# Four re-orderings in a kernel of linear attention and a gated feed-forward block

## Chip and metric

One core of a Trainium2 chip. The metric is the device time of one execution in microseconds, the median of several runs. The engines are TensorE (PE; its weight loads are listed as PEld), VectorE (DVE), ScalarE (ACT), GpSimd (POOL) and SyncE (SP), which here only issues DMAs.

## What is computed

The reference, cut to what matters (8 batches, 8 heads, 576 positions, head size 64; then 4608 tokens, model width 512, hidden width 1536):

```python
def phi(x, c, s):
    r = np.maximum(x, 0.0)
    return np.concatenate([r * c, r * s], axis=-1)
q_p, k_p = phi(q, cos_w, sin_w), phi(k, cos_w, sin_w)
kv = np.einsum('bhsf,bhsd->bhfd', k_p, v)
z = np.sum(k_p, axis=2)
num = np.einsum('bhsf,bhfd->bhsd', q_p, kv)
den = np.einsum('bhsf,bhf->bhs', q_p, z)[..., None] + 1e-06
x = (num / den).transpose(0, 2, 1, 3).reshape(B * S, H * D)

g, val = x @ w_gate, x @ w_val
out = (0.5 * g * (1.0 + erf(g / sqrt(2))) * val) @ w_out
```

## The kernel before

The tokens are taken in nine blocks of 512 (n = 0 to 8), the hidden width in twelve units of 128 columns (jt = 0 to 11, called steps here). A batch has 576 tokens, so a block is made of the end of one batch and the beginning of the next. While the feed-forward part of block n runs, the attention of batch n + 1 is computed in between, and batch n + 2 is loaded and prepared. The order on every engine is the order in which the program is written; the framework only adds the waits.

**Attention of a batch.** `load` brings q, k and v in, two DMAs each, on SyncE's queue (LOADS says in which step). `prep` and `prep_both` multiply the positive part by cosine or sine, one position index j at a time (j = 0 to 8): `prep_both` does q and k in one instruction, on VectorE (L193) or ScalarE (L191). `cast_v` makes v bf16 (L208). `turn_q` transposes q's features with two DMAs (L222). `kv_unit` (L270) sums k times v. `nm_unit` makes the numerators and denominators of one tile of 128 tokens in PSUM banks 6 and 7 (L311), divides on VectorE (denominator L322, reciprocal L323, product into x_sb L324), and `turn_x` transposes x_sb into xT by DMA (L378), in two pieces where a tile falls into two blocks. Tiles that fall into the next block are called late; they are turned in one go. All these transposes, loads and the stores of the output go through SyncE's one queue in the order written. COMING (block 3) and PREPS (blocks 4 to 6) say in which step what is prepared.

**Gate and value.** In blocks 1 to 3, `gv_unit` computes a unit: four matmuls for the gate, GELU on ScalarE (L439), four for the value, and gate times value into hT on VectorE (L442). It alternates between banks 0, 1 and 2, 3. The first `heads` units of a block are done in two halves of 256 columns, all first halves ahead of all second halves, since the block's last columns arrive late. From block 4 on, pairs of units are computed by Strassen's scheme in Winograd's form, with seven products p1 to p7 instead of eight (class `Pair`, matmuls L649). p1 writes a sum bank and ScalarE copies it to another bank (L668); p5 goes to bank 3 (MIX) and is copied to SBUF (L672); p6 is added to the sum bank, and VectorE adds the copy of p5 (L676); p2 and p3 complete the two gates (GELU L681, L685); p7 and p4 complete the two values (L689; products into hT L690, L694). The sums of x that this needs (`x_sum`, L629) are made on GpSimd. Blocks 4 and 5 have four groups each (`group`): one such pair and one ordinary unit, with three steps' worth of other work in between; blocks 6 to 8 have pairs alone (`fast_step`).

**Output.** The output of block n - 1 is computed in the steps of block n (`o_step`), in two parts p of 256 tokens, each by seven products (`product`, matmuls L547) in six steps: products 1 and 2, then 5, 6, 7, 4, 3 (2 and 1 first up to block 3). Products 1, 2, 4, 6 and 7 write bank 4: 1, 6 and 7 accumulate in its left half u, 2 and 4 go to its right half v. Products 5 and 3 write bank 5. After products 1, 6 and 7 ScalarE copies the partial sum u to SBUF (L564), and VectorE adds copies and banks to the output tile (L560). The sums of hT that this needs (`h_sum`, L529) are made on GpSimd from block 4 on.

The order inside a group, with its numerators:

```python
f.p1();  numerators(n, 3 * g);      f.p5();  x()
f.p6();  numerators(n, 3 * g + 1);  f.p2();  y()
f.p3();  f.p7(MIX)
# then an ordinary unit; between its gate and its value:
numerators(n, 3 * g + 2);  z();  f.p4()
```

x, y and z are the steps 3g, 3g + 1 and 3g + 2: an output product, the attention work of the step (where x_sb tiles are turned), and sums on GpSimd.

Of the kernel before, what the change touches and what calls it, by code (L numbers as in the profile page):

```python
# [9 lines left out]
FP32 = mybir.dt.float32  # L10
# [6 lines left out]
def kernel(  # L17
# [13 lines left out]
    nc = tc.nc  # L31
# [6 lines left out]
    JT = J // 128  # L38
# [381 lines left out]
    def gv_unit(n, jt, c0=0, w=BLK, to=None, between=None):  # L420
        xt = xT[n]
        js = slice(jt * 128, (jt + 1) * 128)
        if to is None:
            to = (0, 1) if turn[0] % 2 == 0 else (2, 3)
            turn[0] += 1
        if n not in hT:
            hT[n] = ffn.tile([128, JT, BLK], BF16, name="hT")
        for g, wt in ((0, wg_sb), (1, wv_sb)):
            for ct in range(CT):
                nc.tensor.matmul(  # L430
                    bank(to[g])[:, 0:w],
                    lhsT=wt[:, ct, js],
                    rhs=xt[:, ct, c0:c0 + w],
                    start=(ct == 0),
                    stop=(ct == CT - 1),
                )
            if g == 0:
                gel = ffn.tile([128, BLK], FP32, name="gel")
                nc.scalar.activation(gel[:, 0:w], bank(to[0])[:, 0:w], AF.Gelu)  # L439
                if between:  # L440
                    between()
        nc.vector.tensor_mul(  # L442
            hT[n][:, jt, c0:c0 + w], gel[:, 0:w], bank(to[1])[:, 0:w]
        )
# [36 lines left out]
    JH, CH = JT // 2, C // 2  # L481
# [22 lines left out]
    def place(n, p, name, cols, dtype):  # L504

        if name[0] == "u":
            if n < NB - 1:
                at = {"u1": 0, "u6": 1, "u7": 2}[name] * CH
                return sm[:, at:at + CH]
            rest[0] += CH  # L510
            late = phis.rearrange("p a m r f -> p (a m r f)").bitcast(FP32)
            return late[:, rest[0] - CH:rest[0]]
        at = (int(name[1]) - 1) * JH * 128
        if n < NB - 1:
            return sm[:, 3 * CH:].bitcast(BF16)[:, at:at + JH * 128]
        late = st[:, p].rearrange("p m x -> p (m x)").bitcast(BF16)
        return late[:, at:at + JH * 128]
# [17 lines left out]
    got = {}  # L535
    LEFT, RIGHT = slice(0, CH), slice(CH, C)

    def product(n, p, i, u, m, v):


        a, b = PROD[i]
        key = n, p
        at = {1: u, 6: u, 7: u, 5: m, 3: m, 2: v, 4: v}[i]
        last = n == NB - 1
        joint = not last and n > 2
        for j in range(JH):
            nc.tensor.matmul(  # L547
                at,
                lhsT=hs.setdefault(key, h_parts(n, p))[a][:, j],
                rhs=ts[b][:, j],  # L550
                start=(j == 0 and i in ((1, 2, 4, 5), (1, 4, 5))[joint]),
                stop=(j == JH - 1),
                skip_group_check=i in (3, 6, 7) or joint and i == 2,
            )
        if key not in got:
            got[key] = [outp.tile([128, C], FP32, name="o_sb") for _ in range(2)]
        lo, hi = got[key]

        def add(o, k, x, op=ALU.add):
            nc.vector.tensor_tensor(o, got[key, k], x, op=op)  # L560

        if i in (1, 6, 7) or last and i == 5:
            got[key, i] = place(n, p, f"u{i}", CH, FP32)
            nc.scalar.copy(got[key, i], at)  # L564
        if i == (2 if last or joint else 1):
            add(lo[:, LEFT], 1, v)
        if i == 7:
            add(hi[:, RIGHT], 7, got[key, 5] if last else m)
        if i == 4:
            add(hi[:, LEFT], 7, v, ALU.subtract)  # L570
        if i == 3:
            add(lo[:, RIGHT], 6, m)
        if last and p == 1:

            if i == 2:
                store((nc.sync, nc.sync), 4 * n + p, lo, 0, CH)
            if i == 4:
                store((nc.sync, nc.gpsimd), 4 * n + 2 + p, hi)
            if i == 3:
                store((nc.sync, nc.scalar), 4 * n + p, lo, CH, C)  # L580
        elif i in (3, 4):
            flush()
            stores.append((4 * n + 2 + p, hi) if i == 4 else (4 * n + p, lo))
            if last:
                flush()
# [311 lines left out]
    def js(a, b):  # L897
        return tuple(range(a, b))
# [7 lines left out]
        },  # L906
        3: {
            0: [("k", 4, js(6, 9)), ("v", 4, 0)], 1: [("v", 4, 2)],
            6: [("qk", 5, js(0, 2))], 7: [("qk", 5, js(2, 3))], 8: [("qk", 5, js(3, 5))],
            9: [("v", 5, 0), ("qk", 5, js(5, 6))], 10: [("v", 5, 2), ("qk", 5, js(6, 8))],  # L910
            11: [("qk", 5, js(8, 9))],
        },
    }
    LOADS = {
        (1, 11): [(3, "k"), (3, "v")],
        (2, 1): [(4, "q")], (2, 6): [(4, "k"), (4, "v")],
        (2, 11): [(5, "k")], (3, 1): [(5, "q")], (3, 2): [(5, "v")],
        (3, 9): [(6, "q", 0, 4), (6, "k", 0, 4)],
        (4, 0): [(6, "q", 4, R), (6, "k", 4, R)], (4, 1): [(6, "v")],
        (4, 8): [(7, "q", 0, 4), (7, "k", 0, 4), (7, "v")],  # L920
# [60 lines left out]
    for n in range(1, 4):  # L981
        b = n + 1

        t_kv, t_nm, t_turn = {1: (7, 9, 12), 2: (6, 7, 11), 3: (2, 5, 9)}[n]
        for jt in range(JT):
            if n == 1 and jt >= t_nm:
                nm_unit(2, jt - t_nm, (6, 4, 6)[jt - t_nm])
                turn_x(2, jt - t_nm)
            heads = (0, 2, 4, 2)[n]
            if jt >= heads:  # L990
                gv_unit(n, jt)
            else:
                for i in range(2):
                    half, unit = divmod(2 * jt + i, heads)
                    gv_unit(n, unit, half * HALF, HALF)
                    if n == 1:
                        j = JA + 2 * jt + i
                        prep("q", b, 1, (j,), eng=nc.scalar)
                        prep("q", b, 0, (j,))
                        if jt == i == 0:  # L1000
                            turn_x_pe(1, 3, 5, act_copy)
            if n > 1:
                o_step(n, jt)
            elif jt % 3 == 1:
                flush()
            if n == 1 and jt == 2:
                prep("q", b, 0, (R - 1,))
                prep("q", b, 1, (R - 1,), eng=nc.scalar)
                turn_q(b)
                nm_unit(1, NT - 1)  # L1010
            if n == 1 and jt == 3:
                turn_x(1, NT - 1)
            nms = [(b, jt - t_nm)] if n > 1 and 0 <= jt - t_nm < NT else []
            if n == 2 and jt < 2:
                nms.append((n, 3 + jt))

            i = jt - t_nm - 1
            if n > 1 and 0 <= i < late_of(b):
                turn_x(b, i)
            for bt in nms:  # L1020
                nm_unit(*bt)
            if jt == t_kv:
                kv_unit(b)
            if n == 1 and jt in (2, 3, 4):
                prep_third("k", b, jt - 2)
            if n == 1 and jt == 5:
                cast_v(b, 0, 4, dve_copy)
            if (n, jt) in q3:
                cosines, sines_ = q3[n, jt]
                prep("q", 3, 1, sines_, eng=nc.scalar)  # L1030
                prep("q", 3, 0, cosines)
            for name, c, what in COMING.get(n, {}).get(jt, ()):
                if name == "v":
                    cast_v(c, what, what + 2, dve_copy)
                elif name == "qk":
                    for j in what:
                        prep_both(c, 0, j, nc.scalar if j % 2 else nc.vector)
                        prep_both(c, 1, j, nc.scalar)
                else:
                    prep(name, c, 0, what)  # L1040
                    prep(name, c, 1, what, eng=nc.scalar)
            c = {(2, 1): 2}.get((n, jt), b if n > 1 and jt == t_turn else None)
            if c is not None and n < 3:
                turn_q(c + 1)
            start_loads(n, jt)
            if c is not None:
                for i in range(late_of(c), NT):
                    turn_x(c, i)
            if (n, jt) == (3, JT - 1):
                turn_q(b + 1)  # L1050
            if n == 1 and 4 <= jt < 8:
                wo_sum(("T3", "T1", "T2", "T4")[jt - 4])
            more(n, jt)
# [7 lines left out]
    turns = []  # L1061

    def numerators(n, jt):
        b, t = n + 1, {5: 0, 6: 1, 7: 2, 9: 3, 10: 4}.get(jt)
        if t is not None:
            nm_unit(b, t)
            turns.append((b, t))
# [42 lines left out]
    for n in range(4, NB):  # L1110
# [4 lines left out]
        for i, T in enumerate(pairs):  # L1115
            new = Pair(n, T, 2 * (made % 2), 1, made % 2)
            made += 1
            at = 3 * groups + 2 * i
# [16 lines left out]
    for what in (  # L1135
# [3 lines left out]
        if isinstance(what, str):  # L1139
            p = "ST".index(what[0])  # L1140
# [33 lines left out]
```

## Time and profile before

| | |
|---|---|
| runs | 321.83, 322.48, 325.06 us; median 322.48 |
| the profiled execution | 323.84 us, of which the span is 321.8 |
| busy: PE, PEld | 300.5 us (93%), 222.4 us (69%) |
| busy: DVE, ACT, POOL | 236.3 (73%), 190.1 (59%), 136.9 us (43%) |
| chain of work that ended last, by engine | PE 53%, DMA 19%, DVE 9%, issue 6%, ACT 6%, SP queue 3%, POOL 2% |
| granted TensorE clock | 0.99 |

The page's times are microseconds from the start of the span. Block 3 runs from about 114 to 150, block 4 to 185, block 5 to 219, and blocks 6 to 8 to about 302. A line of a timeline gives start, duration, engine, line, operation, output and inputs, shape, count, and in brackets the idle time before it and what ended that. Matmuls overlap: four of 256 columns are listed with 0.60 us but follow each other every 0.44 us, four of 512 columns every 0.86, and an output product of six takes 0.66.

### The profile page before, as it was taken

How to read it: one execution, taken by the hardware profiler on the slowest of the kernel's cores; microseconds unless marked ns; L12 is line 12 of the kernel's file. 1: busy time of each engine (PE TensorE's matmuls, PEld its weight loads, DVE VectorE, ACT ScalarE, POOL GpSimd, SP SyncE). 2: the span in 40 equal slices, each digit the busy share in tenths (PEclk: the TensorE clock that was granted, in tenths of full speed). 3: DMA queues.
4: the chain of work that ended last, by engine and by line, in shares of the span. 5: the costliest groups of instructions: out<-in, count | busy, mean ns of one | idle time of the engine just before them, and what ended most of it. 6: DMA issues, size and time to landing. Idle time of an engine off the chain costs nothing.

```text
span 321.8 us, 7828 instructions
## 1 busy us (share of the span) xinstructions
PE 300.5 (93%) x3014; PEld 222.4 (69%) x3039; DVE 236.3 (73%) x511; ACT 190.1 (59%) x393; POOL 136.9 (43%) x116
## 2 busy tenths in 40 slices
PE   8799999999999999968998999899999999999993
PEld 3574455654866676635776777677888888888883
DVE  5664887899897996659578947884778765756681
ACT  7664676957473853177566757584555465554631
POOL 5675450000000000008846487747992867296320
PEclk9799999999999999999999999999999999999998
DMA  7999999883799979999799998428641411113035
GB/s 274 229 187 256 298 333 370 250 127 60 248 170 221 346 138 155 294 257 201 92 270 226 322 139 239 84 57 122 94 85 36 89 33 35 42 25 65 3 75 123
DMA packets 71126, 53.66 MB, mean 167 GB/s; under 512 B 45393, under 2 KB 58449, under 8 KB 71089
## 3 DMA queue, kind: packets, MB, share of 16 engines
q1 hardware_dynamic: 61312, 41.17, 56.9%
q0 software_dynamic: 9696, 11.93, 16.0%
q8 instruction: 24, 0.39, 0.5%
q14 instruction: 14, 0.11, 0.1%
q10 hardware_dynamic: 80, 0.07, 0.1%
HBM read 37.75 MB, written 9.44 MB: 147 GB/s over the span
## 4 chain that ended last, share of the span: by engine, by line
PE 53%; DMA 19%; DVE 9%; issue 6%; ACT 6%; SPq 3%; POOL 2%; POOLq 0%; ACTq 0%; DVEq 0%
PE ps L649 22%; PE ps L547 14%; PE ps L430 13%; DMA st<-in_q_dram 7%; DMA wo_sb<-in_moe_w_out_dram 4%; DMA st<-in_v_dram 2%; DMA qT<-phis 2%; DMA wv_sb<-in_moe_w_val_dram 2%; SPq L222 2%; PE ps L311 2%; DVE x_sb L324 2%; DVE hT L442 2%; PE ps L270 2%; DMA xT<-x_sb 1%; ACT sm L564 1%
## 5 line engine op out<-in xcount | busy, mean ns | idle before, releaser
L430 PE MATMUL ps<-xT,wv_sb 128*128 128x512 bf16 (+1 forms) x245 | 56.5, 351 | 0.2
L430 PE MATMUL ps<-xT,wg_sb 128*128 128x512 bf16 (+1 forms) x230 | 54.1, 349 | 1.6 <-DMA xT<-x_sb 0.6
L629 POOL TENSOR_TENSOR fs<-xT 128x512 bf16<-128x512 bf16 x10 | 12.0, 1204 | 99.9 <-DVE phis L193 98.1
L439 ACT ACTIVATE gel<-ps 128x512 f32<-128x512 f32 (+1 forms) x62 | 33.5, 542 | 28.6 <-PE ps L430 26.8
L442 DVE TENSOR_TENSOR hT<-gel,ps 128x512 bf16<-128x512 f32 (+1 forms) x62 | 37.7, 614 | 16.4 <-PE ps L430 13.5
L529 POOL TENSOR_TENSOR sm<-hT 128x768 bf16<-128x768 bf16 x20 | 32.8, 1641 | 30.0 <-PE ps L649 16.3
L430 PEld LDWEIGHTS <-wv_sb 128*128 128x128 bf16 x248 | 24.2, 98 | 20.9
L547 PEld LDWEIGHTS <-sm 128*128 128x128 bf16 x336 | 32.9, 98 | 7.2
L560 DVE TENSOR_TENSOR o_sb<-sm,ps 128x256 f32<-128x256 f32 x56 | 23.3, 417 | 17.5 <-ACT sm L564 13.6
L547 PEld LDWEIGHTS <-hT 128*128 128x128 bf16 x288 | 28.0, 98 | 11.2 <-issue 6.3
L649 PE MATMUL ps<-fs,ws 128*128 128x256 bf16 x240 | 34.5, 273 | 1.2 <-ACT ps L668 1.0
L649 PEld LDWEIGHTS <-ws 128*128 128x128 bf16 x320 | 30.2, 98 | 6.2 <-ACT ps L668 1.7
L689 DVE TENSOR_TENSOR ps<-fs,ps 128x512 f32<-128x512 f32 x26 | 18.1, 695 | 21.7 <-PE ps L649 15.5
L177 ACT ACTIVATE phis<-st,sin_t 128x256 bf16<-128x256 f32 (+1 forms) x75 | 31.5, 483 | 3.2 <-DMA st<-in_q_dram 2.3
L430 PEld LDWEIGHTS <-wg_sb 128*128 128x128 bf16 x248 | 22.6, 98 | 15.5 <-issue 0.5
L649 PE MATMUL ps<-xT,wg_sb 128*128 128x256 bf16 x208 | 31.2, 273 | 0.0
L681 ACT ACTIVATE gel<-ps 128x512 f32<-128x512 f32 x26 | 15.5, 597 | 26.0 <-PE ps L649 26.0
L547 PE MATMUL ps<-wo_sb,hT 128*128 128x256 bf16 x192 | 25.3, 272 | 4.6 <-ACT sm L564 4.6
L324 DVE TENSOR_TENSOR x_sb<-ps,rec 128x512 bf16<-128x512 f32 x38 | 26.3, 691 | 1.3
L685 ACT ACTIVATE gel<-ps 128x512 f32<-128x512 f32 x26 | 15.5, 598 | 12.5 <-PE ps L649 10.0
L547 PE MATMUL ps<-T,sm 128*128 128x256 bf16 x168 | 22.9, 273 | 0.0
L547 PE MATMUL ps<-wo_sb,sm 128*128 128x256 bf16 x168 | 22.9, 273 | 0.0
(123 smaller groups left out, 562.6 us busy)
## 6 DMA issues: line engine op xcount, KB each, us to landing
out_dram<-o_sb SPq DMA_DIRECT2D x69, 128.0 KB, 2.4
st<-in_v_dram SPq DMA_DIRECT2D x12, 576.0 KB, 7.0
st<-in_k_dram SPq DMA_DIRECT2D x8, 576.0 KB, 5.1
st<-in_q_dram POOLq DMA_DIRECT2D x4, 576.0 KB, 12.0
st<-in_q_dram SPq DMA_DIRECT2D x4, 576.0 KB, 4.9
st<-in_q_dram SPq DMA_DIRECT2D x3, 640.0 KB, 5.9
st<-in_q_dram SPq DMA_DIRECT2D x3, 512.0 KB, 4.2
wg_sb<-in_moe_w_gate_dram POOLq DMA_DIRECT2D x6, 256.0 KB, 7.3
```

The costliest lines, as they stand in the source:

```text
L177: nc.scalar.activation(o, i, AF.Relu, scale=tab[:, j:j + 1])
L324: nc.vector.tensor_tensor(x, nm[:, :, :, 0:D], rec[:, :, :, None].to_broadcast([128, 2, 4, D]), op=ALU.mult,)
L430: nc.tensor.matmul(bank(to[g])[:, 0:w], lhsT=wt[:, ct, js], rhs=xt[:, ct, c0:c0 + w], start=(ct == 0), stop=(ct == CT - 1),)
L439: nc.scalar.activation(gel[:, 0:w], bank(to[0])[:, 0:w], AF.Gelu)
L442: nc.vector.tensor_mul(hT[n][:, jt, c0:c0 + w], gel[:, 0:w], bank(to[1])[:, 0:w])
L529: eng.tensor_tensor(a[name][:, j0:j1], a[x][:, j0:j1], a[y][:, j0:j1], op=op)
L547: nc.tensor.matmul(at, lhsT=hs.setdefault(key, h_parts(n, p))[a][:, j], rhs=ts[b][:, j], start=(j == 0 and i in ((1, 2, 4, 5), (1, 4, 5))[ ...
L560: nc.vector.tensor_tensor(o, got[key, k], x, op=op)
L649: nc.tensor.matmul(to[:, 256 * half:256 * half + 256], lhsT=w_part(a, j * 128, (j + 1) * 128)[:, ct], rhs=xb[self.n][b][:, ct], start=(hal ...
L681: nc.scalar.activation(self.gel0, self.other, AF.Gelu)
L685: nc.scalar.activation(gel1, bank(MIX), AF.Gelu)
L689: nc.vector.tensor_tensor(bank(val), self.m5, self.sum, op=ALU.add)
```

## The change

It has four parts, and touches no size and no type.

```diff
@@ product
-        if i in (1, 6, 7) or last and i == 5:
-            got[key, i] = place(n, p, f"u{i}", CH, FP32)
-            nc.scalar.copy(got[key, i], at)
+        if i in (6, 7) or i == (2 if joint else 1) or last and i == 5:
+            k, of = (1, u) if i == 2 else (i, at)
+            got[key, k] = place(n, p, f"u{k}", CH, FP32)
+            nc.scalar.copy(got[key, k], of)
@@ COMING and LOADS
-            6: [("qk", 5, js(0, 2))], 7: [("qk", 5, js(2, 3))], 8: [("qk", 5, js(3, 5))],
-            9: [("v", 5, 0), ("qk", 5, js(5, 6))], 10: [("v", 5, 2), ("qk", 5, js(6, 8))],
-            11: [("qk", 5, js(8, 9))],
+            5: [("qk", 5, js(0, 1))], 6: [("qk", 5, js(1, 2))], 7: [("qk", 5, js(2, 4))],
+            8: [("v", 5, 0), ("qk", 5, js(4, 5))], 9: [("v", 5, 2), ("qk", 5, js(5, 7))],
+            10: [("qk", 5, js(7, 9))],
-        (2, 11): [(5, "k")], (3, 1): [(5, "q")], (3, 2): [(5, "v")],
+        (2, 11): [(5, "k")], (3, 0): [(5, "q")], (3, 1): [(5, "v")],
@@ the loop over blocks 1 to 3
-            heads = (0, 2, 4, 2)[n]
+            heads = (0, 2, 4, 4)[n]
             if jt >= heads:
-                gv_unit(n, jt)
+                gv_unit(n, jt, to=(2, 6) if (n, jt) == (3, JT - 1) else None)
...
             start_loads(n, jt)
+            c = {(2, 1): 2, (3, 2): 3, (3, 9): 4}.get((n, jt))
             if c is not None:
                 for i in range(late_of(c), NT):
                     turn_x(c, i)
@@ numerators (blocks 4 and 5)
-        b, t = n + 1, {5: 0, 6: 1, 7: 2, 9: 3, 10: 4}.get(jt)
+        b, t = n + 1, {5: 0, 7: 1, 8: 2, 10: 3, 11: 4}.get(jt)
```

1. **Copy.** For the outputs of blocks 3 to 7 (`joint`; ten parts) the copy of the first sum u is issued behind product 2 instead of between products 1 and 2.
2. **Loads.** Batch 5's q and v are loaded one step earlier (steps 0 and 1 of block 3), and the late tiles of batch 3 are turned in step 2 of block 3 instead of step 11 of block 2. On SyncE's queue the order after batch 5's k was: two late transposes, a store of two DMAs, q, v. It is now: q, the store, v, the two late transposes. The preparation of batch 5 begins in step 5 instead of 6 and ends in step 10 instead of 11; v's casts move from steps 9 and 10 to 8 and 9.
3. **Block 3's units.** Four units instead of two are done in halves. The last unit (11) writes banks 2 and 6 instead of 0 and 1.
4. **Numerators.** In blocks 4 and 5 the five tiles are done in steps 5, 7, 8, 10, 11 instead of 5, 6, 7, 9, 10. On SyncE's queue tile 4's transpose moves from ahead of a store to just ahead of the transpose of the next batch's q.

GpSimd's order of instructions stays as it was. TensorE has 16 matmuls more.

## The prediction

> **What bounds the kernel now.** I read first the list of TensorE's waits: engine, line, releaser, total us, times, longest.
>
> ```profile
> PE ps L547 <- ACT sm L564: 4.6, 10, 0.5
> PE ps L311 <- DVE x_sb L324: 3.5, 3, 2.8
> ...
> PE ps L649 <- ACT ps L668: 1.0, 1, 1.0
> ...
> PE ps L430 <- DMA xT<-x_sb: 0.6, 2, 0.3
> ```
>
> These four come to 9.7 us, and each is touched by a part of the change. (p1 to p7 are the seven products of a pair of hidden units, products 1 to 7 those of the output.) Whether a wait's removal reaches the end shows in the busy time by stretch (PE, weight loads, DVE, ACT, POOL, clock, DMA share, GB/s):
>
> ```profile
> 140.00:160.00 20.00, 16.05 (x183) 10.98 (x185) 15.36 (x28) 14.32 (x28) 13.20 (x9) 1.00 0.90 167
> ...
> 200.00:220.00 20.00, 18.86 (x171) 14.41 (x171) 17.23 (x38) 13.26 (x24) 10.11 (x8) 1.00 0.39 84
> ...
> 260.00:280.00 20.00, 19.54 (x180) 17.29 (x178) 13.88 (x25) 11.12 (x21) 8.60 (x8) 1.00 0.19 40
> ```
>
> From 222 us TensorE is the only full engine; in blocks 4 and 5 (150 to 219) VectorE is close behind; at 140 to 160 nobody is full, so something is waited for. TensorE's timeline (start, duration) shows the waits:
>
> ```profile
> 117.61 0.60 PE L430 MATMUL ps<-xT,wg_sb 128*128 128x256 bf16 x4 [0.28 <-DMA xT<-x_sb]
> ...
> 142.40 0.42 PE L311 MATMUL ps<-kv_sb,qT 128*128 128x65 bf16 x8 [2.76 <-DVE x_sb L324]
> ...
> 152.08 0.61 PE L649 MATMUL ps<-fs,ws 128*128 128x256 bf16 x4 [0.99 <-ACT ps L668]
> ...
> 236.32 0.82 PE L547 MATMUL ps<-wo_sb,hT 128*128 128x256 bf16 x6
> 237.59 0.82 PE L547 MATMUL ps<-wo_sb,hT 128*128 128x256 bf16 x6 [0.46 <-ACT sm L564]
> ```
>
> The last two lines are output products 1 and 2, with one of the ten 0.46 us waits between them.
>
> The chain of waits behind the 2.76 us, and SyncE's queue ahead of it:
>
> ```profile
> 132.49 5.57 DMA st<-in_q_dram
> ...
> 138.79 1.32 ACT phis L191 x2
> 140.11 0.49 ACT gel L439
> ```
> ```profile
> 125.39 1.89 SPq L98 DMA_DIRECT2D st<-in_k_dram  x2
> 127.41 3.13 SPq L378 DMA_TRANSPOSE xT<-x_sb  x2
> 130.59 1.22 SPq L453 DMA_DIRECT2D out_dram<-o_sb  x2
> 131.92 1.05 SPq L98 DMA_DIRECT2D st<-in_q_dram  x2
> ```
>
> Batch 5's q lands at 138.06. The feature preparation waits for it in the queues of ScalarE and VectorE, and a GELU and a numerator stand behind it there.
>
> The profiled execution took 323.84 us: span 321.8, 2.04 around it. The median of the runs is 322.48, 1.36 less. I sum against 323.84 and carry the difference to the median.
>
> **The copy of the first sum.** Products 1 and 2 write the two halves of one PSUM bank; product 2 now waits until the copy (0.37 us) has read the first half. The copy moves behind product 2. The next write to the copied half is product 6, two steps later, so nobody on TensorE waits for it there; on ScalarE the GELU of p3 is queued behind, whose matmuls end 0.44 us after product 2, when the copy is done. The vector add behind the copy loses nothing: before, it could start at 0.46 + 0.66 = 1.12 us after product 1, now at 0.66 + 0.42 = 1.08. What is late next for product 2 is its fifth matmul, which reads the last hidden tiles of the block: VectorE ends them at 252.28, and that matmul would start at 252.13 + 0.44 = 252.57. It fits. Ten waits of 0.46: six from 221 us on count in full (2.76), two in the first groups of blocks 4 and 5, where VectorE idles (0.92); the two in their third groups are counted with the numerators. Sum 3.7.
>
> **Batch 5's q.** Its two loads pass two transposes and go out after k's, at 127.3 and 127.9 instead of 131.9 and 132.5. Bounds of the landing: 127.9 + 5.1 (k's own time) = 133.0, and 127.9 + 8.6 (the slowest v load there) = 136.5. I take 134.2: k and q together are 2.36 MB, and the two best slices here moved 388 and 371 GB/s, which is 6.2 us from 128, when the transposes of batch 4's q let go. The store, v and the late transposes follow, these to about 134 instead of 130.5; they land within the 8.6 too, and their first reader is POOL's x sum at 144.84.
>
> But the first preparation also moves a step earlier, from step 6 to 5, where VectorE arrives at 132.5 and ScalarE at 130.2. After the landing come sine 0.72, GELU 0.49, product into hT 0.60, output add 0.33, a Strassen sum 0.47, and 0.08 + 0.24 + 0.70 for the numerator: 3.6. TensorE wants the bank back at 136.84, so a landing after 133.2 makes it wait, one for one. At 134.2: 1.0 instead of 2.76. Gain 1.75 (0 to 2.76).
>
> **Unit 11 in banks 2 and 6.** Block 4's first copy (L668, p1 into bank 1) no longer waits for unit 11's hT (151.38). It then follows its own matmuls: copy 0.57 + 0.1, of which 0.44 lies beside p5, so 0.25 of the 0.99 stays. ScalarE now carries three preparations (3 x 0.62) beside GELU and copy in steps 9 and 10, 2.6 us in a step of 2.64; I charge 0.15 for unit 10's GELU, since unit 11 wants its bank. Gain 0.6 (0 to 0.99). With no preparation left in step 11, q's transpose for batch 5 starts earlier than 153.5.
>
> **Four halved units.** 16 matmuls more, but eight of 256 columns take 0.88 us and four of 512 take 0.86: 4 x 0.02 = 0.08 us. GELU grows by 4 x 0.39 - 2 x 0.59 = 0.4 and the hT products by 4 x 0.416 - 2 x 0.683 = 0.3; VectorE's 2.31 us of idle at 125.76 hides that, and without it the 0.3 would go to TensorE. The wait at 117.61 goes (0.45 from piece to piece), yet VectorE is busy without a gap from 117.77 to 123.4, and TensorE meets the first value bank, returned at 120.4, 0.4 early. Net 0 (-0.4 to 0.45).
>
> **Numerators further apart.** The waits of 0.38 go, once per block. With the copy, the third group of block 4 runs 1.0 us ahead and the fourth 1.3 to 1.5. But tile 4's numerator (1.0 us on VectorE) now stands in the fourth group in front of the hT product L694, which releases the copy L668 and through it the next block's p6:
>
> ```profile
> 218.80 0.57 ACT L668 COPY ps<-ps 128x512 f32<-128x512 f32 x1 [1.19 <-DVE hT L694]
> ```
>
> Block 4: numerator to 182.8, output add and two preparations to 184.0, L694 to 184.65, copy to 185.35, against p6 at 186.20 before: 0.85. Block 5, the same way: preparations to 217.9, L694 to 218.55, p6 at 219.25 against 219.42: 0.17. Sum 1.0, between 2 x (0.38 + 0.46 + 0.46) = 2.6, all waits of the two groups with nothing behind them, and -0.5, where the numerator's 1.0 us in block 5 finds only half its cover in the idle that VectorE has there. SyncE's transpose of q follows tile 4's: 0.6 us later at 185, landing about 197.1, while its reader moves from 198.42 to about 197.2: free by a hair. POOL's x sums (176.07) start up to 2 us later; their first reader in block 5 is at 185.2, after their end at 182.6.
>
> **A rule beside the rows.** The preparation L193 took 0.48 us at 142.27 with POOL idle, 1.37 and 1.74 at 149.40 and 151.63 with POOL at work; the casts of v took 0.83 and 0.78 at 147.02 and 148.70, against 0.75 elsewhere. So two preparations stay slow and the casts stay as they are. The Trainium skill (SBUF — State Buffer, Who interferes with whom) says that VectorE in two-port modes, casts among them, and GpSimd exclude each other for a whole instruction; by that step 9's cast would be held too, the 0.6 of unit 11 would be lost, and the sum would be 6.45.
>
> **Sum.** 3.7 + 1.75 + 0.6 + 0 + 1.0 = 7.05: 316.8 against the profiled 323.84, and 322.48 - 7.05 = 315.4 as a median.
>
> **Rivals.**
> 1. q lands no earlier in effect (136 or later) and VectorE limits blocks 4 and 5 to their present ends: only the 3.7 and some of the 0.6 stay. For it: VectorE has 2.1 us of idle in the last groups of block 5, half of it behind a GELU. Against: the two loads are issued 4.6 us earlier. 322.48 - 4.2 = 318.3.
> 2. The copies' removal is replaced: product 2 waits for VectorE's hT, or the change doesn't take the wait away. For it: product 2 carries a wait on VectorE already. Against: the 0.29 us computed above. Left are 1.75 + 0.6 + 1.0 = 3.35, or 319.1; with rival 1 as well, 322.
> 3. Slower: the preparation stands in the queues too early. From step 5 on it blocks GELU and hT for as long as q is not there; each us of landing after 133.2 costs one. It outweighs the rest (3.7 + 0.6 + 1.0 + 2.76 = 8.1) from a landing at 141.3 on; at 145 the time is 326. Against: 141.3 is 13.4 us after issue, and the slowest load here took 8.6.
> 4. Better: landing by 133 and the group gains in full: 2.76 + 0.99 + 0.45 + 2.6 + 3.7 = 10.5, or 312.
>
> **Numbers.** Forecast 0.62, rival 1 0.18, rival 2 0.07, rival 3 0.05, rival 4 0.08. A measurement of this kernel can't tell less than about 1% (3.2 us) from no change. Faster by more: forecast, rivals 1 and 4, and a third of rival 2, less some for the spread of the runs (321.83 to 325.06): 0.86. Same 0.09, slower 0.05. Range 313.0 to 319.0: it leaves out the far part of rival 4, rival 3 and most of rival 2.
>
> **What would show it.** The ten waits on the copy gone from TensorE's list; q issued near 127.5 and a wait at a numerator in step 7 of block 3 of about 1 us; p6 at the start of block 4 waiting about 0.25, that of block 6 still behind L694. A wait of product 2 on VectorE, or of numerators on the transposed q, would make the prediction wrong.

## The result, and the profile after

The changed kernel took 320.83 us (median of 19 runs, 317.63 to 323.98); the kernel before took 324.20 beside it (19 runs, 321.13 to 326.46). The ratio is 0.988, 95% interval 0.9845 to 0.9914: faster by 3.9 us, plus or minus 1.1, where 7.05 was forecast. The ratio goes by the fast runs alone and leaves out those more than 1.5% above the fastest of their kernel (5 of 19 after, 3 of 19 before). The direction was right and the range (313 to 319) was not. Part of the miss is the base: the three runs shown before had a median of 322.48, the 19 have 324.20. The profiled executions are 323.84 and 318.62 us, 5.22 apart.

TensorE's waits after, from the list of waits (engine, line, releaser, total us, times, longest; lines from 565 on are one higher than before):

```profile
PE ps L650 <- ACT ps L669: 2.4, 5, 1.0
PE ps L311 <- DVE x_sb L324: 2.1, 1, 2.1
...
PE ps L311 <- DMA qT<-phis: 0.9, 2, 0.7
...
PE ps L650 <- DVE ps L677: 0.5, 1, 0.5
```

The ten waits on the copy of the first sum are gone, and no other wait of an output product has come. New is the first row: p6 waits for the copy of p1 five times instead of once. The third row is new too; its longest wait, 0.65, is for batch 7's transposed q. The same places in TensorE's timeline:

```profile
139.77 0.42 PE L311 MATMUL ps<-kv_sb,qT 128*128 128x65 bf16 x8 [2.12 <-DVE x_sb L324]
...
151.63 0.61 PE L650 MATMUL ps<-fs,ws 128*128 128x256 bf16 x4 [0.22 <-ACT ps L669]
...
184.56 0.61 PE L650 MATMUL ps<-fs,ws 128*128 128x256 bf16 x4 [0.96 <-ACT ps L669]
...
217.65 0.61 PE L650 MATMUL ps<-fs,ws 128*128 128x256 bf16 x4 [0.52 <-ACT ps L669]
...
230.80 0.40 PE L311 MATMUL ps<-kv_sb,qT 128*128 128x65 bf16 x7 [0.65 <-DMA qT<-phis]
...
234.75 1.47 PE L547 MATMUL ps<-wo_sb,hT 128*128 128x256 bf16 x12
```

The last line is output products 1 and 2 in one piece: twelve matmuls in 1.47 us. Busy time by stretch (PE, weight loads, DVE, ACT, POOL, clock, DMA share, GB/s):

```profile
140.00:160.00 20.00, 19.63 (x215) 13.34 (x212) 15.49 (x29) 13.64 (x26) 13.54 (x9) 1.00 0.83 154
...
200.00:220.00 20.00, 18.67 (x178) 14.58 (x177) 17.75 (x34) 13.22 (x24) 11.90 (x9) 1.00 0.41 85
...
260.00:280.00 20.00, 20.00 (x186) 17.85 (x185) 13.04 (x24) 11.57 (x22) 9.76 (x9) 1.00 0.25 54
```

From 260 to 280 TensorE is full (19.54 before). From 200 to 220, the last part of block 5, it is less busy than before (18.67 against 18.86).

Batch 5's q, from SyncE's queue and from the chain of waits:

```profile
125.58 2.00 SPq L98 DMA_DIRECT2D st<-in_k_dram  x2
127.71 1.58 SPq L98 DMA_DIRECT2D st<-in_q_dram  x2
129.33 1.19 SPq L453 DMA_DIRECT2D out_dram<-o_sb  x2
130.61 1.46 SPq L98 DMA_DIRECT2D st<-in_v_dram  x2
```
```profile
128.82 7.02 DMA st<-in_q_dram
...
135.95 0.04 ACT phis L191
...
136.58 0.58 ACT gel L439
```

The first load is issued 4.2 us earlier than before, as intended. The second starts at 128.82 instead of 132.49, 3.7 us earlier (the forecast was 127.9); it takes 7.02 us instead of 5.57 and lands at 135.84, 2.22 us earlier.

In the following, the time is divided at p6 of blocks 4, 5 and 6 (152.08, 185.75 and 219.42 before; 151.63, 184.56 and 217.65 after) and at the end of TensorE's work (316.81 and 312.14). Up to p6 of block 4 the change wins 0.45 us, in block 4 0.74, in block 5 0.58, in blocks 6 to 8 2.90, and 0.55 behind TensorE's end and around the span: 5.22. The first of these is the least certain. TensorE's order is the same in all kernels up to block 3, yet block 3's first matmul starts at 114.10 before and at 114.66 after, and between 113.1 and 115.9 over all the profiled executions.

### The profile page after: what moved, and what is told of

The parts are those of the page before. It is cut to its first block, busy times and chain, and to the rows that moved or that the text cites. A ratio compares the mean times of both kernels' runs of the same rounds, so it can differ in the third digit from the quotient of the medians.

```text
span 316.8 us, 7876 instructions
## 1 busy us (share of the span) xinstructions
PE 300.1 (95%) x3055; PEld 223.2 (70%) x3055; DVE 236.8 (75%) x513; ACT 189.5 (60%) x395; POOL 135.7 (43%) x116
## 4 chain that ended last, share of the span: by engine, by line
PE 49%; DMA 24%; DVE 10%; ACT 6%; issue 6%; POOL 1%; SPq 1%; POOLq 0%; ACTq 0%; DVEq 0%
PE ps L650 18%; PE ps L547 14%; PE ps L430 13%; DMA st<-in_q_dram 6%; DMA qT<-phis 5%; DMA wo_sb<-in_moe_w_out_dram 4%; DMA wg_sb<-in_moe_w_gate_dram 2%; DMA st<-in_v_dram 2%; DMA xT<-x_sb 2%; DVE x_sb L324 2%; PE ps L270 2%; DMA wv_sb<-in_moe_w_val_dram 2%; PE ps L311 2%; DVE ps L690 2%; DVE hT L691 2%
## 5 line engine op out<-in xcount | busy, mean ns | idle before, releaser
L430 PE MATMUL ps<-xT,wg_sb 128*128 128x512 bf16 (+1 forms) x256 | 57.2, 346 | 0.7 <-DMA xT<-x_sb 0.5
L430 PE MATMUL ps<-xT,wv_sb 128*128 128x512 bf16 (+1 forms) x256 | 57.2, 346 | 0.3 <-DVE hT L442 0.3
L430 PEld LDWEIGHTS <-wv_sb 128*128 128x128 bf16 x256 | 25.0, 98 | 20.6 <-issue 0.5
L430 PEld LDWEIGHTS <-wg_sb 128*128 128x128 bf16 x256 | 23.4, 98 | 15.3 <-DMA xT<-x_sb 0.7
L682 ACT ACTIVATE gel<-ps 128x512 f32<-128x512 f32 x26 | 15.5, 597 | 24.6 <-PE ps L650 24.5
L565 ACT COPY sm<-ps 128x256 f32<-128x256 f32 x42 | 15.6, 372 | 16.2 <-PE ps L547 15.8
L547 PE MATMUL ps<-wo_sb,hT 128*128 128x256 bf16 x192 | 23.7, 273 | 0.0
```

Of the source, the lines that this page charges most:

```text
L430: nc.tensor.matmul(bank(to[g])[:, 0:w], lhsT=wt[:, ct, js], rhs=xt[:, ct, c0:c0 + w], start=(ct == 0), stop=(ct == CT - 1),)
L547: nc.tensor.matmul(at, lhsT=hs.setdefault(key, h_parts(n, p))[a][:, j], rhs=ts[b][:, j], start=(j == 0 and i in ((1, 2, 4, 5), (1, 4, 5))[ ...
L565: nc.scalar.copy(got[key, k], of)
L682: nc.scalar.activation(self.gel0, self.other, AF.Gelu)
```

## Experiments

The first four take one part of the change each; theory A is that each part is worth what its rows say, the others that something takes it back. All ratios are to the kernel before.

**The copy alone**

```diff
-        if i in (1, 6, 7) or last and i == 5:
+        if i in (6, 7) or i == (2 if joint else 1) or last and i == 5:
```

(with the two lines under it, as in the change)

> The kernel before, with the copy of the first sum behind product 2 and nothing else. Theory A (the copies' waits are worth what their row says, and the shortfall lies in the other parts): all ten waits gone, the six from 221 us on in full, the two in the third groups partly lost to VectorE: 3.7 to 4.6 us less, ratio 0.986 to 0.989. Theory B (the removed copies come back as other waits, and the gain of the whole change is from block 3): 2 us or less, ratio 0.994 or more.

Measured: 0.9854 (0.9806 to 0.9903), 4.7 us less: theory A or a little more, and by the middle values more than the whole change, though the intervals overlap.

**Batch 5's q alone**

```diff
-        (2, 11): [(5, "k")], (3, 1): [(5, "q")], (3, 2): [(5, "v")],
+        (2, 11): [(5, "k")], (3, 0): [(5, "q")], (3, 1): [(5, "v")],
```

(with the preparations a step earlier and the late tiles in step 2, as in the change)

> The kernel before, with only the loads, the late transposes and the preparation of batch 5 moved. Theory A: q is issued 4 us earlier but takes 7 us to land, and the preparation stands one step earlier in its queues, so the wait at a numerator of block 3 shrinks from 2.76 to about 2.1 us and moves a step ahead: 0.3 to 0.8 us less, ratio 0.997 to 1.0. Forecast as written: 1.75 us less, 0.9945. Theory C (early preparation in front of GELU costs more in executions where q lands later): 1 us or more slower, 1.003 or more.

Measured: 1.0019 (0.9986 to 1.0052). At most 0.5 us can have been won; the forecast was 1.75. Between theories A and C this does not decide.

**The numerators alone**

```diff
-        b, t = n + 1, {5: 0, 6: 1, 7: 2, 9: 3, 10: 4}.get(jt)
+        b, t = n + 1, {5: 0, 7: 1, 8: 2, 10: 3, 11: 4}.get(jt)
```

> The kernel before, with only the numerators of blocks 4 and 5 spread. Theory A: the two waits of 0.38 us go, but the last numerator stands before the product into hT that releases the next block's first copy, and the transposed q of batch 7 lands late: between 0.5 us less and 0.5 us more, ratio 0.9985 to 1.0015. Theory D (this part takes back what the others gain): 1.5 us or more slower, 1.005 or more.

Measured: 1.0007 (0.9965 to 1.0048), as in theory A. The waits of 0.38 are gone, and five waits of p6 on the copy of p1 stand there (2.7 us).

**The units alone**

```diff
-            heads = (0, 2, 4, 2)[n]
+            heads = (0, 2, 4, 4)[n]
-                gv_unit(n, jt)
+                gv_unit(n, jt, to=(2, 6) if (n, jt) == (3, JT - 1) else None)
```

> The kernel before, with four halved units in block 3 and its last unit in banks 2 and 6. Theory A: the wait of 0.99 us at the start of block 4 falls to about 0.2, the wait for the transposed x at 117.6 goes but VectorE takes most of it back: 0.6 to 1.0 us less, ratio 0.997 to 0.998. Rival: the preparations left in step 11 and their q transpose hold block 4 instead, 0.3 us or less, 0.999 or more.

Measured: 0.9939 (0.9886 to 0.9992). p6 of block 4 waits 0.23 instead of 0.99, as forecast; but in the runs of the copy alone and of the numerators alone it waits 0.23 too, so the ratio cannot be put down to this wait.

If the copy alone is worth more than everything, something in the change costs time. The next four look for it.

**q of batch 5 on GpSimd's queue**

```diff
         for b, name, *part in LOADS.get((n, jt), ()):
-            if part:
+            if (b, name) == (5, "q"):
+                for m in (0, 2):
+                    load(nc.gpsimd, name, b, m, m + 2)
+            elif part:
```

> The changed kernel with one edit: the two loads of batch 5's q go out on GpSimd's queue, which is idle from 46 to 144 us, instead of behind the two transposes of batch 4's q and behind k on SyncE's; they should be issued between 116 and 126 us and land by 131 instead of 135.84. Theory A (the late landing cost what the prediction missed in block 3): the 2.12 us wait of the numerator in step 7 of block 3 falls to below 0.5 and the end of TensorE's work comes 1.5 us earlier; ratio to the kernel before 0.983 against 0.988 for the change. Theory B (blocks 4 and 5 end where VectorE lets them, so time won in block 3 isn't kept): the wait falls just as far, the third product's start in block 4 moves by 1 to 1.7 us, but TensorE's last work by less than 0.5; ratio 0.987. Theory C (transfers in parallel with the transposes hold each other up): the wait stays above 1 us, since q or the transposes land later; ratio 0.988 or above.

Measured: 0.9864 (0.9833 to 0.9895), the same as the change. Theory C comes nearest. The two transposes that now ran beside a load took SyncE's queue 12.77 us instead of 8.42 (SyncE's timeline, then the chain, of this run):

```profile
115.68 12.77 SPq L222 DMA_TRANSPOSE qT<-phis  x2
128.49 2.39 SPq L98 DMA_DIRECT2D st<-in_k_dram  x2
```
```profile
130.51 5.52 DMA st<-in_k_dram
```

so k was issued 2.9 us later and landed at 136.03, about when q had landed in the change (135.84); the preparation takes both.

**The change without the part on q**

```diff
-        (2, 11): [(5, "k")], (3, 0): [(5, "q")], (3, 1): [(5, "v")],
+        (2, 11): [(5, "k")], (3, 1): [(5, "q")], (3, 2): [(5, "v")],
```

(and the preparations and late tiles as before)

> The changed kernel without the part on batch 5's q (loads, preparations and late transposes stand where they stood before); the copies, the numerators and the halved units are changed. Theory A (that part is worth what the landing says, 2.76 - 2.12 = 0.6 us): ratio to the kernel before 0.990. Theory B (time won in block 3 is lost in blocks 4 and 5): 0.988, as the change. Theory C (the early preparation stands in the way of GELU and hT products, here 5.1 us of ScalarE's wait for q): faster than the change, 0.984 or below.

Measured: 0.9838 (0.982 to 0.9855), not slower than the change. This agrees with theory C. q lands at 138.05, 2.2 us later than in the change, and p6 of block 4 starts at 151.31, 0.3 earlier.

**The change without the part on the numerators**

```diff
-        b, t = n + 1, {5: 0, 7: 1, 8: 2, 10: 3, 11: 4}.get(jt)
+        b, t = n + 1, {5: 0, 6: 1, 7: 2, 9: 3, 10: 4}.get(jt)
```

> The changed kernel without the part on the numerators (they stand at steps 5, 6, 7, 9, 10 again). By the prediction's terms this part is worth 1.0 us together with the copies of the third groups: ratio 0.991, with waits of 0.38 back at the third group of every block and with p6 of blocks 4 and 5 where they were. Theory D (the later numerators push the fifth tile's transpose, and q's behind it, so that batch 7's q lands late by 0.65 us and p6 waits 0.35 at blocks 5 and 6): without them that 0.65 goes, and the time is 0.5 to 1 us below the change's: 0.985 to 0.9865. Theory B: no difference to the change, 0.988.

Measured: 0.9811 (0.9772 to 0.985), some 2.2 us below the change: theory D, and more than it said.

**The copy and the units together**

> The kernel before with only two parts: the copy behind the second output product, and the four halved units with unit 11 in banks 2 and 6. By the sum of the single runs (4.8 us for the copies, 2.0 for the units, of some 325): 0.979. By the prediction's rows (3.7 + 0.6, and up to 0.9 for the copies in the third groups): 0.984 to 0.987. Theory B (nothing before block 6 is kept, only the copies in blocks 6 to 8 count, 6 x 0.46 = 2.76): 0.9915, and then what the copy alone gave over that is spread of the runs.

(The diffs of the first and the fourth run.) Measured: 0.9817 (0.9794 to 0.984), 5.9 us less: two parts of the change are worth more than all four. Theory B falls.

What is lost where can be read once block 4 is reached (us from one of the marks above to the next):

| | block 4 | block 5 | blocks 6 to 8 |
|---|---|---|---|
| before | 33.67 | 33.67 | 97.39 |
| copy alone | 32.50 | 32.49 | 93.67 |
| numerators alone | 34.16 | 34.16 | 97.39 |
| the change | 32.93 | 33.09 | 94.49 |
| the change without the numerators | 32.50 | 32.48 | 93.67 |
| the copy and the units | 33.05 | 32.49 | 94.01 |

The copies' gain is the same with and without the other parts (second and fifth row); the last row departs by 0.55 in block 4, where a numerator waits 1.30 us for batch 5's transposed q (more on that below). The copies are worth 1.17, 1.18 and 3.72: 6.07 us for ten, 0.61 each, more than the 4.22 that the whole change wins from p6 of block 4 on. The numerators cost 0.49 in each of blocks 4 and 5 without the copies; with them 0.43, 0.60 and 0.82: 1.85. The 0.82 is the late transposed q of batch 7. Theory D was then sharpened: what costs is a numerator in the last step of a group (8 and 11). VectorE's timeline and ScalarE's at the end of block 4 in the changed kernel:

```profile
181.44 0.69 DVE L324 TENSOR_TENSOR x_sb<-ps,rec 128x512 bf16<-128x512 f32 x1
182.04 0.41 DVE L560 TENSOR_TENSOR o_sb<-sm,ps 128x256 f32<-128x256 f32 x1
182.37 0.88 DVE L193 TENSOR_SCALAR phis<-st,cos_t 128x512 bf16<-128x512 f32 x2
183.16 0.68 DVE L695 TENSOR_TENSOR hT<-gel,ps 128x512 bf16<-128x512 f32 x1
```
```profile
183.93 0.57 ACT L669 COPY ps<-ps 128x512 f32<-128x512 f32 x1 [2.22 <-DVE hT L695]
```

The numerator's three instructions stand before the hT product L695, the copy of p1 waits 2.22 us for that, and p6 (184.56, above) for the copy.

**Only step 8, not 11**

```diff
-        b, t = n + 1, {5: 0, 7: 1, 8: 2, 10: 3, 11: 4}.get(jt)
+        b, t = n + 1, {5: 0, 7: 1, 8: 2, 9: 3, 10: 4}.get(jt)
```

> The changed kernel with the numerators at steps 5, 7, 8, 9, 10 (10 and 11 go back to 9 and 10; only step 8 is the last of a group of three). Theory D, sharpened by the run with the numerators undone (a numerator in the last step of a group stands before the hT product L695, whose end releases the copy L669 that the next group's p6 waits for): p6 of the third group still waits 0.35, p6 of blocks 5 and 6 waits at most 0.2 instead of 0.96 and 0.52, blocks 4 and 5 take 32.0 to 32.5 us from p6 to p6 instead of 32.93 and 33.09, and q of batch 7 is transposed 0.6 us earlier, so that the 0.65 wait in block 6 goes: 2 us faster than the change, ratio to the kernel before 0.982. Theory B (VectorE's sum of work sets blocks 4 and 5, wherever the numerators stand): p6 to p6 within 0.15 of 32.93 and 33.09, ratio 0.987.

Measured: 0.977 (0.9721 to 0.982); blocks 4 and 5 take 32.41 each and blocks 6 to 8 93.67, in all 2.0 us less than in the change. In its timelines the hT product ends earlier, the copy no longer waits for it, and p6 waits for nothing:

```profile
183.55 0.57 ACT L669 COPY ps<-ps 128x512 f32<-128x512 f32 x1 [1.05 <-PE ps L650]
```
```profile
184.18 0.61 PE L650 MATMUL ps<-fs,ws 128*128 128x256 bf16 x4
```

**Only step 11, not 8**

```diff
-        b, t = n + 1, {5: 0, 7: 1, 8: 2, 10: 3, 11: 4}.get(jt)
+        b, t = n + 1, {5: 0, 6: 1, 7: 2, 9: 3, 11: 4}.get(jt)
```

> The changed kernel with the numerators at steps 5, 6, 7, 9, 11 (only tile 4's is moved, to the last step of the fourth group). Theory D: the waits of p6 at blocks 5 and 6 stay (0.7 to 1.0 and 0.4 to 0.6), the 0.38 of the third groups is back, the 0.35 of the third groups' p6 is gone; p6 to p6 takes 33.2 to 33.5 us in both blocks, longer than in the change; q of batch 7 still lands late; ratio 0.990. Theory B: 32.5 to 32.9, since the third group has lost nothing; ratio 0.985.

Measured: 0.9896 (0.9847 to 0.9946); blocks 4 and 5 take 33.28 and 33.36, and p6 waits 0.81 and 0.51 at their ends. By blocks, both runs lie within what theory D gave. But the two last steps of a group are not alike. A numerator in step 8 costs nothing in the end: p6 of the third group waits 0.35 us for it, the wait of 0.38 is gone, and the block takes 32.41 against 32.50 without the part on the numerators. A numerator in step 11 alone makes the block 0.8 to 0.9 us longer.

**The change without the copy part**

```diff
-        if i in (6, 7) or i == (2 if joint else 1) or last and i == 5:
+        if i in (1, 6, 7) or last and i == 5:
```

(with the lines under it as before)

> The changed kernel with the copy of the first sum back in front of the second output product. If a removed wait is worth its row (0.46): ten are back, 4.6 us, of which blocks 4 and 5 may hide some; ratio to the kernel before 1.002 or less. If it is worth what the starts of products 1 and 2 show (1.27 us apart with the wait, 0.65 without: 0.62 each): 3.7 us in blocks 6 to 8 and 1.2 in each of blocks 4 and 5, 6.2 in all; ratio 1.007, blocks 4 and 5 at 34.1 to 34.2 us from p6 to p6, blocks 6 to 8 at 97.4 less nothing. If the copies were replaced by other waits in blocks 4 and 5: below 0.999.

Measured: 1.0013 (0.9974 to 1.0052), below the 1.007 of the second case; blocks 4 and 5 at 34.17 and 34.16 and blocks 6 to 8 at 97.47 are as that case said. From p6 of block 4 on it takes 5.29 us more than the change: the copies' 6.07 less the 0.82 of the late transposed q, which now has cover. The ratios of this run and of the change are 1.35% apart, 4.3 us, less than these 5.29 but within their intervals.

**q without v beside it**

```diff
-        (2, 11): [(5, "k")], (3, 0): [(5, "q")], (3, 1): [(5, "v")],
+        (2, 11): [(5, "k")], (3, 0): [(5, "q")], (3, 3): [(5, "v")],
```

(and v's casts in steps 9 and 10, with the preparations of steps 8 to 10 dealt out anew around them)

> The changed kernel with batch 5's v loaded after the late transposes of x instead of right behind q (v's casts at steps 9 and 10, as before), so that q shares the DMA engines with k, a store and transposes alone. Theory A (q landed at 135.84 instead of 134.2 because v's 1.2 MB ran beside it): q lands 5.0 to 5.8 us after issue, near 134, the wait of the numerator in step 7 falls from 2.12 to 0.5 to 1.2, p6 of block 4 comes 1 us earlier; ratio 0.985. Theory E (k in front of it and the end of q's transposes set the landing): still 6.5 to 7.5 us, wait 2 or more; ratio 0.988. If v then lands after step 9's turn: the casts stand in the way, GELU or hT product wait, ratio 0.990 or above.

Measured: 0.9856 (0.9812 to 0.9901). The ratio is near theory A's and its interval holds both, but the profile has what theory E said: q still took 7.53 us from issue to landing, and the numerator waited 2.29. So v is not what makes q late. Between 128 and 136 us of the changed kernel the DMA engines moved 334, 340, 301 and 403 GB/s in steps of 2 us, and up to the landing at 135.84 that is 2.69 MB: k and q (2.36), the store between them (0.26) and little else.

So q cannot land much earlier behind the transposes, yet 2.2 us earlier ought to be worth something. In the two runs with the units and without the part on q, p6 of block 4 came 13.26 us after the landing, in both; in the change, in the two with other numerators and in the one without the copies it came 15.79 after it, in all four. (Executions in which the clock fell in between are left out; see the last section.) The next run takes the two halves of that part apart, with the numerators at 5, 7, 8, 9, 10.

**Loads early, preparations where they were**

```diff
-            5: [("qk", 5, js(0, 1))], 6: [("qk", 5, js(1, 2))], 7: [("qk", 5, js(2, 4))],
-            8: [("v", 5, 0), ("qk", 5, js(4, 5))], 9: [("v", 5, 2), ("qk", 5, js(5, 7))],
-            10: [("qk", 5, js(7, 9))],
+            6: [("qk", 5, js(0, 2))], 7: [("qk", 5, js(2, 3))], 8: [("qk", 5, js(3, 5))],
+            9: [("v", 5, 0), ("qk", 5, js(5, 6))], 10: [("v", 5, 2), ("qk", 5, js(6, 8))],
+            11: [("qk", 5, js(8, 9))],
```

> The changed kernel with the numerators at steps 5, 7, 8, 9, 10 and with batch 5's preparations at the steps where they were before, while its loads stay early. Theory F (the early landing is worth something, and the early preparation gives it back): q lands near 136.0 as in the run with the same numerators, but p6 of block 4 follows 13.3 us after it or by TensorE's own work, 34.4 us after block 3's first matmul (35.45 less a wait of 1.06 in the run without this part), so near 149.1 instead of 151.77; the wait of a numerator in block 3 falls below 0.3; blocks 4 and 5 take 32.4 from p6 to p6; ratio to the kernel before 0.971. Theory G (block 3 ends by something else, such as VectorE's or ScalarE's pile of preparations at its end): p6 of block 4 within 0.5 of 151.77, or waits of more than 1 us on hT or GELU in steps 9 to 11; ratio 0.977.

Measured: 0.9737 (0.9697 to 0.9777), the fastest of all: 315.85 us against 324.18, and 1.4% below the change by the two ratios. Of that, 1.1% came with the numerators (0.977 above); the step from there to 0.9737 is 0.3% and lies within the intervals. What shows the effect of the order is the profile. ScalarE's timeline around the landing in the changed kernel, and in this run:

```profile
130.24 0.60 ACT L439 ACTIVATE gel<-ps 128x512 f32<-128x512 f32 x1 [1.78 <-PE ps L430]
135.95 0.72 ACT L191 ACTIVATE phis<-st,sin_t 128x512 bf16<-128x512 f32 x1 [5.12 <-DMA st<-in_q_dram]
136.58 0.58 ACT L439 ACTIVATE gel<-ps 128x512 f32<-128x512 f32 x1
```
```profile
133.12 0.60 ACT L439 ACTIVATE gel<-ps 128x512 f32<-128x512 f32 x1 [2.04 <-PE ps L430]
135.30 0.37 ACT L565 COPY sm<-ps 128x256 f32<-128x256 f32 x1 [1.58 <-PE ps L547]
136.73 0.72 ACT L191 ACTIVATE phis<-st,sin_t 128x512 bf16<-128x512 f32 x1 [1.06 <-DMA st<-in_q_dram]
```

In the change a GELU and a copy of the same step wait behind the preparation; here they are done before it, and ScalarE waits 1.06 us instead of 5.12. The numerator waits 0.44 and p6 of block 4 starts at 149.90, 13.2 us after q's first use instead of 15.7 (135.95 to 151.63), although q came 0.8 us later than in the change.

**Neither half, with the same numerators**

```diff
-        b, t = n + 1, {5: 0, 6: 1, 7: 2, 9: 3, 10: 4}.get(jt)
+        b, t = n + 1, {5: 0, 7: 1, 8: 2, 9: 3, 10: 4}.get(jt)
```

(on the kernel before, with the diffs of the first and the fourth run)

> The kernel before with the copies, the halved units with unit 11 in banks 2 and 6, and the numerators at steps 5, 7, 8, 9, 10; nothing of batch 5's q is changed. Theory F: q lands near 138.1, p6 of block 4 13.3 us later, at 151.3 to 151.5: the same as with the whole part on q (151.77) within 0.5, and 2.2 later than with the loads alone; ratio 0.977. Theory G: the same as both, 0.977. If the part on q as a whole is worth its forecast 1.75 us: 0.982.

Measured: 0.9856 (0.9814 to 0.9898): slower than expected, and 1.2% above the run before. In the profiled execution everything ahead of q on SyncE's queue ran 2 us later (q is issued at 133.91, before at 131.92) and q lands at 140.24; p6 of block 4 follows at 155.18, 14.9 us later instead of 13.3, and batch 5's transposed q makes a numerator wait 1.51 us at 168.93. The 1.6 us agree with a fall of the clock (1.7 us, last section). That transposed q is what theory F had left out. In the three executions with the copies and the units but without the part on q its transpose is issued 2.1 to 2.8 us after p6 of block 4, and a numerator waits 0.64, 1.30 and 1.51 us for it; with the loads early it is issued 1.3 us after p6 (0.6 with the preparations early too), and no such wait of more than 0.2 is seen there. How the 1.2% divide among clock, transposes and spread was not settled.

The part on q as a whole was measured in four pairs of ratios, with it against without it: alone (1.0019 against 1), in the change (0.988 against 0.9838), with the numerators where they were (0.9811 against 0.9817) and with them at 5, 7, 8, 9, 10 (0.977 against 0.9856). It comes out slower in two, level in one and faster in one: no gain that can be told from the spread.

## Why the prediction was off

The mechanism of the copies was right and their size too low; the term of the numerators failed, and that of batch 5's q was mis-sized. By terms, with profiled times (the copies and the numerators by the table of blocks):

| term | forecast | measured |
|---|---|---|
| eight copies | 3.7 | 4.86 (8 x 0.607) |
| numerators, with the copies of the third groups | 1.0 | -0.64 (4.22 in all from p6 of block 4 on, less 4.86) |
| batch 5's q, unit 11, halved units | 2.35 | 0.45 |
| behind TensorE's end, around the span | 0 | 0.55 |
| sum | 7.05 | 5.22 |

**Copies: mis-sized, low.** The step charged each wait at the 0.46 that the list of waits shows. That is idle time after an end, and a product of six matmuls is listed with 0.82 us while the next starts after 0.66. The two starts that the prediction itself quoted, 236.32 and 237.59, are 1.27 apart; without the wait they are 0.65 apart: 0.62 each, and 0.61 was measured. The Trainium skill (Perfetto Trace Analysis, Tensor Engine Instruction) says that the end of a TensorE instruction is estimated by the profiler and not observed; the rows agree. That nothing else would hold product 2 (rival 2) was right.

**Numerators: the step that failed.** The prediction saw that tile 4's numerator stands before L694 and that the next p6 waits for that, and yet forecast a gain: 0.85 and 0.17. It set p6 after (185.35) against 186.20, but p6 of block 5 starts at 185.75 before; 186.20 is p2, the matmul behind it:

```profile
185.75 0.61 PE L649 MATMUL ps<-fs,ws 128*128 128x256 bf16 x4
186.20 0.60 PE L649 MATMUL ps<-xT,wg_sb 128*128 128x256 bf16 x4
```

That alone takes 0.45 off the 0.85. And what is left is the gain of all of block 4, so it already holds the first group's copy (0.46), which stands among the 3.7 too. What the runs show in place of a gain: with the copies in place, the new steps of the numerators cost 1.85 us (0.43, 0.60 and 0.82), and tile 4's place in step 11 is what costs. The same blocking at step 8 (p6 of the third groups, 0.35) it did not look for; that one is paid for by the wait of 0.38 that goes. The late transpose of q, "free by a hair" at block 5, was late by 0.65 at block 6, where tile 4's transpose stands before q's on SyncE's queue; start to start that cost 0.82. Its lower bound of -0.5 was not low enough.

**Batch 5's q: the landing mis-sized.** The landing was put at 134.2 from 2.36 MB at 380 GB/s; 2.69 MB at 343 GB/s went by up to 135.84, inside the bounds (133.0 to 136.5) but near the bad one. From the landing on the working holds: 3.6 us to the numerator gives 139.4, and it came at 139.77. The price of the earlier preparation was in the prediction too, one for one from 133.2 on: with the landing at 135.84 its own rule leaves 2.76 - 2.64 = 0.1 of the 1.75. The runs show a little less than that: the landing is 2.22 earlier, but p6 of block 4 follows 15.79 us behind it and not 13.26, so 0.3 is lost. That is near nothing, as in rival 1. What the prediction did not weigh is to move the loads alone: with the preparation left where it was, p6 of block 4 came 13.2 us after q and 1.9 us earlier (149.90 against 151.77), in one profiled execution each.

**Unit 11** did what was forecast (p6 waits 0.22 instead of 0.99); the 0.45 of the table is this 0.77 less the 0.3 of batch 5's q. **The halved units** left a wait of 0.33 on an hT product at 121.06 in place of that at 117.61, as near nothing as forecast. **The casts of v** took 0.76 us at 143.91 and 0.87 at 147.84 in the changed kernel, so the 0.6 that the prediction weighed was not lost. But that was luck of timing: that a sum running on GpSimd holds a cast on VectorE back does show. The second cast ends at 148.71, 0.62 after the sum on GpSimd that was under way when it was issued (146.94 to 148.09). In the run of batch 5's q alone a cast was issued just behind the start of such a sum (143.52 to 144.67), and ends 0.63 after it:

```profile
143.61 1.69 DVE L208 CAST vx<-st 128x1152 bf16<-128x1152 f32 x1
```

In all the profiled executions a cast of batch 5's v that was issued while one of these sums ran ended 0.61 to 0.67 us after that sum did, and took 0.75 to 1.71 us, against 0.75 or 0.76 beside an idle GpSimd.

## What to carry over

Price a TensorE stall by the distance of starts with and without it, not by the idle time listed. Before an instruction is moved in a queue, ask what waits behind it at the new place: a numerator in step 11 cost more than the wait that its move took away, and a preparation ahead of its data took back the 2.2 us that the data came earlier. Issue a transfer earlier by itself first, and move its consumer only when the landing is known.

## What was not expected of the hardware

The wait for q in block 3 can cost more than its length. In six of the sixteen profiled executions the granted clock fell to half close to the end of that wait, from 0.6 us before it to 1.3 us after it. TensorE's timeline and the busy time by stretch (the clock is the third number from the end) in the last run:

```profile
144.58 0.47 PE L311 MATMUL ps<-kv_sb,qT 128*128 128x65 bf16 x8 [3.27 <-DVE x_sb L324]
144.86 1.90 PE L430 MATMUL ps<-xT,wg_sb 128*128 128x512 bf16 x4
```
```profile
142.00:144.00 2.00, 0.00 (x0) 0.00 (x0) 1.13 (x4) 2.00 (x5) 0.00 (x0) 1.00 3.00 279
144.00:146.00 2.00, 1.42 (x11) 0.71 (x11) 1.93 (x6) 1.97 (x4) 0.00 (x0) 0.70 0.18 15
146.00:148.00 2.00, 2.00 (x5) 0.76 (x5) 0.96 (x2) 0.60 (x1) 0.00 (x0) 0.50 0.82 254
148.00:150.00 2.00, 1.80 (x19) 1.24 (x18) 1.18 (x3) 0.90 (x3) 1.22 (x2) 0.95 1.11 342
```

Here the clock is 1.00 while TensorE idles and falls when it works again; four matmuls then take 1.90 us instead of 1.02. In the run of the copy alone it fell while TensorE still idled (at 144.4, and TensorE worked again from 145.05 on). In all six the loss adds up to 1.7 us (here 0.30 x 2 + 0.50 x 2 + 0.05 x 2), which is half the clock for 3.4 us. The waits before it were 2.02, 2.71, 2.93, 2.96, 3.27 and 3.74 us; after 2.76 in the kernel before, 2.12 in the changed one and even 3.16 in the run without the copy part there was no fall. The Trainium skill (TensorE: Matmul & The Clock Gate, What's actually happening) has the same halving, over a window of about 3.4 us that runs free of the kernel; it asks for an idle window, and here five of the six waits were shorter than that and were enough. Falls of the same size stand at 10 to 16 us of four executions, that of the kernel before among them; at block 3's first matmul no loss from them can be seen (114.10 before, 114.66 after). The falls can be part of why the runs of one kernel lie some 5 us apart: over the 29 runs of the kernel before that stand beside the first four experiments, time and granted clock go against each other (correlation -0.71). That a kernel without the wait should scatter less fits the run with late preparations (314.75 to 316.69), but was not tested by itself.
